# Sequence matrices stored as pairs of tiles: one 512 KB load for two tiles in the first mixing layer of an FNet and GEGLU stack

## The chip, the cores and the metric

The kernel runs on one core of one Trainium2 chip. The metric is the device time of one execution in microseconds (us). Lines named L126 and the like are lines of the kernel before; lines of the changed kernel are said to be such.

## What is computed

Four layers on x (2048 rows of 512 numbers, float32), each added to its input after a layer norm without weights: a Fourier mixing, a GEGLU feed-forward, and both once more.

```python
def _A_ref(x, dft_seq_re, dft_seq_im, dft_hid_re, dft_hid_im):
    a = jnp.einsum("bsd,ed->bse", x, dft_hid_re)
    b = jnp.einsum("bsd,ed->bse", x, dft_hid_im)
    y = jnp.einsum("ts,bse->bte", dft_seq_re, a) - jnp.einsum("ts,bse->bte", dft_seq_im, b)
    return y
def _B_ref(x, w_gate, w_up, w_down):
    return (_gelu(x @ w_gate) * (x @ w_up)) @ w_down
...
x = x + _A_ref(_layernorm(x, axis=-1), ...)   # layer 0
x = x + _B_ref(_layernorm(x, axis=-1), ...)   # layer 1
x = x + _A_ref(_layernorm(x, axis=-1), ...)   # layer 2
x = x + _B_ref(_layernorm(x, axis=-1), ...)   # layer 3
```

The sequence matrices are 2048 by 2048, the hidden ones 512 by 512; the feed-forward is 1792 wide.

## The kernel before

**Products.** Every float32 operand is split in two: ScalarE (ACT) rounds it to a high part (L126), VectorE (DVE) subtracts that from the operand and leaves a low part (L128). A product is then three matmuls, high by high, high by low and low by high (`mm3`, L166 to L168). Most have 512 columns. On top of it the large products run by Winograd's scheme, seven block products for eight, so DVE also forms sums and differences of blocks (`plus`, L157, and `minus`, L154). In layers 0 and 2 the left matrix has the real sequence matrix above the imaginary one, cut at half the sequence: A11 and A12 are the two halves of the real one, A21 and A22 those of the imaginary one. The right matrix is the normed x, cut at half the sequence and at half the features.

**Slots.** SBUF has 93 places of 128 by 512 floats (`Slots`, handed out by `sb.get`, given back by `sb.put`), each the tile of one operand. PSUM has eight banks.

**Sequence tiles.** The host cuts each sequence matrix into tiles of 128 (sequence, on the partitions) by 512 (output rows, a block `b` of four). In DRAM (`ws`) a tile lies in one piece of 256 KB, 2 KB on each partition. `items` is the list of all operands in the order in which TensorE (PE) will want them; `load_next` (L302 is its DMA) takes slots for the next item and starts its loads on the queue of SyncE (SP), some items ahead of the split.

**The first stage of layer 0** (`FORE`, run by `fore`) multiplies all four blocks at once with each of the 16 row tiles `j` of x: for each `j` four sequence tiles, each split and used in six matmuls, 24 matmuls a `j`, in eight PSUM banks. In the first eight `j` it is A11 with the first half of x; then A12 with the second half. Meanwhile the rows of x come in (L194) and are normed: statistics on DVE (L531 to L536), with a power on GpSimd (POOL, L535), and the scaling on ACT (L572). After that, block by block, come the stages `S2` (which loads A21 and A22 of the same `k` in one item and sums them, `make_s2`) and `S4`, and the hidden products between them. Layers 1 and 3 (`geglu`) read split weights from DRAM (`wb`, `wc`): they were split in the first layers and stored, seven halves to a row of 14 KB, so that a tile that is read back is a cut of 2 KB from each such row.

**Order.** The code records operations one after another; a scheduler then sets the order on each engine by its own estimates of time, gives out buffers and inserts the waits. Any change of a load can so move instructions on all engines. SP has eight completion counters for its transfers, and a transfer that has to wait for a buffer holds up those behind it on SP.

## Time and profile before

| | us |
|---|---|
| median of 3 runs | 1589.22 (1588.48 to 1590.95) |
| the profiled execution | 1589.32 |
| its span, first to last instruction | 1587.3 |
| PE busy | 1579.0 |
| DVE busy | 1250.1 |
| ACT busy | 875.4 |
| POOL busy | 253.6 |

The span is what the profile's instructions cover; 2.0 us of the execution's time lie around it. TensorE's granted clock is full through nearly all of the span. DMA moved 427.04 MB, 269 GB/s on the mean. A row such as `12.71 0.50 PE L166 ... [0.75 <-ACT s L126]` reads: started at 12.71 us, took 0.50 us, and the engine sat idle 0.75 us before it until an ACT instruction of line 126 released it. Matmuls overlap: each shows about 0.39 us, and they start some 0.23 us apart. In order listings a tile is named by its place or kind and a running number: `s_735` is a slot's tile, `d_613` a tile of a pair in the changed kernel, `p` a PSUM bank, and `wide` and `xwide` are four-slot tiles that are lent out as slots.

### The profile page before, as it was taken

The page shows a single profiled execution, that of the slowest core. Times are in us where ns is not written, and L with a number is a line of the kernel's source. Part 1 is how long each engine was busy: PE and PEld are TensorE (multiplying, and loading weights), DVE is VectorE, ACT ScalarE, POOL GpSimd, SP SyncE. Part 2 cuts the span into 40 slices and gives each one's busy share as a digit, 9 for nine tenths or more (in the row PEclk, how much of TensorE's full clock was granted, in tenths as well). Part 3 has the DMA queues.
Part 4 walks back from the last instruction along what each step waited for, and adds up shares of the span by engine and source line. Part 5 has one row for each costly group of instructions (what it writes and reads, how often), then busy time and mean ns, then how long its engine had stood idle before and what let it go on. Part 6 is the DMA issues. An engine that isn't in the chain of part 4 may idle for free.

```text
span 1587.3 us, 23208 instructions
## 1 busy us (share of the span) xinstructions
PE 1579.0 (99%) x7000; PEld 1307.6 (82%) x7000; DVE 1250.1 (79%) x2174; ACT 875.4 (55%) x1714; POOL 253.6 (16%) x445
## 2 busy tenths in 40 slices
PE   9999999999999999999999999999999999999998
PEld 7888888888888888888888888888888888888887
DVE  8999999889699795566969997869985458754475
ACT  7864574645676652746768444566546435433361
POOL 2200324311465201230031000021002000000001
PEclk9999999999999999999999999999999999999999
DMA  9946989987999999996976785789998967896463
GB/s 360 332 150 232 361 270 362 335 286 259 328 344 345 297 329 301 288 331 221 310 238 217 270 229 172 233 283 309 279 327 239 297 198 238 293 289 197 135 197 81
DMA packets 257660, 427.04 MB, mean 269 GB/s; under 512 B 33344, under 2 KB 89408, under 8 KB 256512
## 3 DMA queue, kind: packets, MB, share of 16 engines
q1 hardware_dynamic: 228560, 333.28, 66.2%
q0 software_dynamic: 26544, 91.51, 15.7%
q8 instruction: 55, 0.90, 0.2%
q10 hardware_dynamic: 2432, 0.79, 0.2%
q14 instruction: 69, 0.57, 0.1%
HBM read 335.02 MB, written 90.44 MB: 268 GB/s over the span
## 4 chain that ended last, share of the span: by engine, by line
PE 96%; DVE 2%; DMA 2%; issue 0%; ACT 0%; SPq 0%; DVEq 0%; ACTq 0%
PE p L166 32%; PE p L167 32%; PE p L168 32%; DMA s<-ws 1%; DVE s L128 1%; DVE s L154 0%; DMA s<-x 0%; DVE s L157 0%; DVE xwide L154 0%; ACT s L126 0%; DVE wide L154 0%; SPq L302 0%; SPq L194 0%; ACT s L572 0%; DVE wide L157 0%
## 5 line engine op out<-in xcount | busy, mean ns | idle before, releaser
L167 PE MATMUL p<-s,s 128*128 128x512 f32 x2326 | 899.8, 388 | 0.0
L168 PE MATMUL p<-s,s 128*128 128x512 f32 x2326 | 887.6, 388 | 0.0
L166 PE MATMUL p<-s,s 128*128 128x512 f32 x2326 | 872.5, 388 | 2.0 <-ACT s L126 1.5
L126 ACT ACTIVATE s<-s 128x512 fp32r<-128x512 f32 (+1 forms) x868 | 487.4, 608 | 319.8 <-DVE s L154 108.7
L128 DVE TENSOR_TENSOR s<-s,s 128x512 fp32r<-128x512 f32 (+1 forms) x868 | 546.0, 669 | 58.2 <-ACT s L126 54.0
L166 PEld LDWEIGHTS p<-s,s 128*128 128x128 f32 x2326 | 436.7, 188 | 94.2 <-ACT s L126 3.4
L167 PEld LDWEIGHTS p<-s,s 128*128 128x128 f32 x2326 | 436.8, 188 | 89.7 <-DVE s L128 0.5
L168 PEld LDWEIGHTS p<-s,s 128*128 128x128 f32 x2326 | 436.6, 188 | 89.4
L157 DVE TENSOR_TENSOR s<-s,p 128x512 f32<-128x512 f32 (+1 forms) x293 | 196.2, 682 | 189.6 <-PE p L168 109.5
L154 DVE TENSOR_TENSOR s<-s,s 128x512 f32<-128x512 f32 (+1 forms) x414 | 249.8, 623 | 2.8 <-DMA s<-ws 0.9
L161 ACT ACTIVATE s<-p 128x512 f32<-128x512 f32 x252 | 146.9, 592 | 147.0 <-PE p L168 142.0
L1079 ACT ACTIVATE s<-s 128x512 f32<-128x512 f32 x112 | 70.3, 629 | 121.5 <-DVE s L157 121.0
L247 POOL DMA_DIRECT2D x<-wide x16 | 10.4, 660 | 374.7 <-DVE wide L157 374.7
L285 POOL DMA_DIRECT2D wb<-s x84 | 45.9, 548 | 100.2 <-ACT s L126 73.3
L1093 DVE TENSOR_TENSOR s<-s,s 128x512 f32<-128x512 f32 x84 | 57.9, 689 | 1.9
L126 ACT ACTIVATE s<-xwide 128x512 fp32r<-128x512 f32 (+1 forms) x52 | 31.0, 613 | 27.5 <-DVE xwide L157 10.0
L572 ACT ACTIVATE s<-s,shift,rstd 128x512 f32<-128x512 f32 x55 | 44.0, 807 | 3.9 <-DVE shift L536 3.2
L157 DVE TENSOR_TENSOR s<-s,s 128x512 f32<-128x512 f32 (+1 forms) x68 | 40.1, 591 | 5.0 <-DMA s<-wgu 3.3
L545 POOL TENSOR_SCALAR rstd<-rstd 128x1 f32<-128x1 f32 x48 | 14.2, 296 | 179.9 <-ACT junk L544 179.1
L285 POOL DMA_DIRECT2D wc<-s x42 | 30.1, 718 | 74.8 <-ACT s L126 53.2
L128 DVE TENSOR_TENSOR s<-xwide,s 128x512 fp32r<-128x512 f32 (+1 forms) x52 | 35.0, 682 | 7.1 <-ACT s L126 7.0
L542 ACT ACTIVATE junk<-s 128x512 f32<-128x512 f32 x45 | 28.1, 623 | 18.7 <-DMA s<-x 18.4
(105 smaller groups left out, 526.8 us busy)
## 6 DMA issues: line engine op xcount, KB each, us to landing
s<-ws SPq DMA_DIRECT2D x348, 256.0 KB, 5.1
s<-wb SPq DMA_DIRECT2D x294, 256.0 KB, 5.4
s<-wc SPq DMA_DIRECT2D x196, 256.0 KB, 4.5
wb<-s POOLq DMA_DIRECT2D x98, 256.0 KB, 5.6
s<-wp SPq DMA_DIRECT2D x56, 256.0 KB, 4.0
wc<-s POOLq DMA_DIRECT2D x49, 256.0 KB, 5.7
s<-x SPq DMA_DIRECT2D x45, 256.0 KB, 5.3
xwide<-x SPq DMA_DIRECT2D x43, 256.0 KB, 8.0
```

The costliest lines, as they stand in the source:

```text
L126: nc.scalar.activation(hi, src, AF.Copy)
L128: nc.vector.tensor_tensor(lo, src, f32(hi), op=ALU.subtract)
L154: nc.vector.tensor_tensor(out, a, b, op=ALU.subtract)
L157: nc.vector.tensor_tensor(out, a, b, op=ALU.add)
L161: nc.scalar.activation(v, src, AF.Copy)
L166: nc.tensor.matmul(ps, ah, bh, start=start, stop=False, skip_group_check=True)
L167: nc.tensor.matmul(ps, ah, bl, start=False, stop=False, skip_group_check=True)
L168: nc.tensor.matmul(ps, al, bh, start=False, stop=stop, skip_group_check=True)
L285: nc.gpsimd.dma_start(to, t)
L572: nc.scalar.activation(z, x, AF.Identity, bias=shift, scale=rstd)
L1079: nc.scalar.activation(t, g, AF.Gelu_apprx_tanh)
L1093: nc.vector.tensor_tensor(t, t, v, op=ALU.mult)
```

## The change

**In DRAM** the host now lays sequence tiles in pairs: `wf` holds, for the first stage, blocks 0 and 1 (and 2 and 3) of one `j` side by side, 4 KB on each partition; `ws` holds for the real matrix the tiles `k` and `k+1` of a block side by side, and for the imaginary one A21 and A22 of the same `k`. Each is a view of 128 by 1024.

**In SBUF** four pairs of slots (`Pairs`, `d0` to `d3`) take the place of eight slots. The halves of a pair are handed out singly too, but while `sb.reserved` is set (the first stage from `j` = 6 on, and the rest of layer 0) other requests take them last. `get_two` hands out both halves of a free pair where there is one, for float32 alone.

**Loads.** From `j` = 6 on the first stage, and the A21 and A22 item of `S2` in layer 0, go through `Twin`: with a free pair, one transfer of 512 KB fills both tiles; without one, two transfers of 256 KB read the two halves of the view. Everything else reads half a view: 2 KB from each 4 KB. Split weights and hidden weights that happen to lie in the two halves of a pair are joined as well (`kept`, `piece_load`, `load_next`). Of SP's 1493 transfers 36 are saved: 14 joined loads from `wf`, 21 from `ws`, and one of a feed-forward weight. DVE, ACT, PE and POOL's DMAs keep their numbers of instructions.

```diff
+NPAIR = 4
+RESERVE_AT = 6
+JOINED_FROM = 6
...
+    class Pairs(Slots):
+        def __init__(self, pool, n, pairs):
+            super().__init__(pool, "s", n - 2 * pairs)
+            self.free += [(i, h) for i in range(pairs) for h in range(2)]
+            self.kinds, self.reserved = {}, False
...
+            fit = [n for n in self.free if fits(n)]
+            n = next((n for n in fit if not (self.reserved and self.paired(n))), fit[0])
...
+        def get_two(self, dtype=F32):
+            whole = [n for at, n in enumerate(self.free) if self.paired(n) and n[0] not in self.kinds and (n[0], 1 - n[1]) not in self.free[at + 1:]]
+            if dtype != F32 or not whole:
+                return self.get(dtype), self.get(dtype)
+            return self.half_of((whole[0][0], 0), dtype), self.half_of((whole[0][0], 1), dtype)
...
+    class Twin:
+        def __init__(self, view):
+            self.view, self.tiles = view, []
+        def load(self, i):
+            if not self.tiles and not i:
+                self.tiles = list(sb.get_two())
+                both = sb.joined(*self.tiles)
+                for to, a in zip((both,) if both is not None else self.tiles, (self.view,) if both is not None else halves(self.view)):
+                    stream["last"] = nc.sync.dma_start(to, a)
+            return self.tiles[i]
...
-                    for c in range(FORE[layer]):
-                        raw(plain, ws[c * 2 * NS + j])
+                    for c in range(0, FORE[layer], 2):
+                        view = wf[c // 2, j]
+                        two = halves(view) if j < JOINED_FROM else ((twin := Twin(view), 0), (twin, 1))
+                        for a in two:
+                            raw(plain, a)
...
+            low = [Twin(ws[b * NS + NK + k]) for k in range(NK)]
+            high = [a for k in range(NK) for a in halves(ws[b * NS + k])]
+            a11, a12 = high[:NK], high[NK:]
+            a21, a22 = ([halves(twin.view)[i] if layer else (twin, i) for twin in low] for i in range(2))
...
             for j in range(NS):
+                sb.reserved = j >= RESERVE_AT
...
+        sb.reserved = layer == 0 and NPAIR > 0
```

On SP, in the first stage, these rows stand in a row before (the loads from `ws` are the sequence tiles of `j` = 6 and 7, those from `x` rows of x):

```order
L302 DMA s_413<-ws 128x512
L302 DMA s_438<-ws 128x512
L302 DMA s_463<-ws 128x512
L302 DMA s_478<-ws 128x512
L194 DMA s_450<-x 128x512
L194 DMA s_425<-x 128x512
L302 DMA s_496<-ws 128x512
L302 DMA s_521<-ws 128x512
L302 DMA s_536<-ws 128x512
L194 DMA s_508<-x 128x512
```

And now, from the same row of the queue on (L398 and L194 of the changed kernel are `load_next` and `Twin.load`, L273 is the load of a row of x):

```order
L398 DMA s_413<-wf 128x512
L398 DMA s_438<-wf 128x512
L194 DMA d_463<-wf 128x1024
L273 DMA s_450<-x 128x512
L273 DMA s_425<-x 128x512
L194 DMA d_494<-wf 128x1024
L273 DMA d_506<-x 128x512
L194 DMA s_530<-wf 128x512
L194 DMA s_531<-wf 128x512
L273 DMA s_567<-x 128x512
```

The two loads of a pair have become one row twice as wide; a row of x has taken half of the fourth pair, and the next two sequence tiles (`s_530`, `s_531`) are therefore loaded singly. Up to here the order of loads is that of before.

On PE, where `j` = 8 begins (second half of x, first bank `p1`), the order before is as follows; the first name behind the arrow is the part of the sequence tile, the second that of x:

```order
L168 MATMUL p0_232<-s44_727,s31_654 128x512
L166 MATMUL p1_225<-s51_745,s84_490 128x512
L167 MATMUL p1_225<-s55_746,s84_490 128x512
L168 MATMUL p1_225<-s51_745,s84_490 128x512
L166 MATMUL p1_225<-s74_835,s21_613 128x512
```

And now:

```order
L247 MATMUL p0_232<-s42_715,s26_646 128x512
L245 MATMUL p1_225<-s44_735,s82_488 128x512
L245 MATMUL p2_226<-s44_735,s82_488 128x512
L246 MATMUL p1_225<-s61_736,s82_488 128x512
L247 MATMUL p1_225<-s44_735,s82_488 128x512
```

The second matmul of the tile (its low part, `s_746` before, `s_736` now) is put one matmul later. It stands at row 195 of PE's list before and at row 196 now.

On DVE the low part `s_746` stands at row 86 of before:

```order
L531 BN_STATS st<-s_548 128x6
L536 SCALAR_TENSOR_TENSOR shift<-mv,rstd 128x1
L128 TENSOR_TENSOR s_746<-s_619,s_745 128x512
L128 TENSOR_TENSOR s_771<-s_642,s_770 128x512
L533 BN_AGGR mv<-st 128x2
```

The low part `s_736`, of the first joined tile of `j` = 8, stands at row 121 now (L207 of the changed kernel is L128 of before, L233 is L154, L632 to L637 are the statistics):

```order
L632 BN_STATS st<-s_786 128x6
L233 TENSOR_TENSOR s_937<-s_436,s_937 128x256
L207 TENSOR_TENSOR s_809<-s_797,s_809 128x256
L207 TENSOR_TENSOR s_812<-s_797,s_812 128x256
L634 BN_AGGR mv<-st 128x2
L233 TENSOR_TENSOR s_940<-s_436,s_937 128x256
L233 TENSOR_TENSOR s_1055<-s_332 128x256
L635 TENSOR_SCALAR rstd<-mv 128x1
L207 TENSOR_TENSOR s_736<-d_613,s_735 128x512
L233 TENSOR_TENSOR s_1058<-s_672,s_332 128x256
L207 TENSOR_TENSOR s_759<-d_613,s_758 128x512
```

Statistics, splits of rows of x and first differences of x, which before stood behind it, now stand ahead of it: 35 more of DVE's rows come before the low part that PE needs first in `j` = 8. From row 77 to row 121 there are now 5 splits of 512 columns, 12 of 256, 5 differences of 256, 5 statistics (BN_STATS), 6 BN_AGGR, 6 TENSOR_SCALAR and 6 SCALAR_TENSOR_TENSOR.

More of the change, by code (lines that the diff above doesn't have):

```diff
@@ new lines, in fnet_geglu @@
+    class Twin:
[8 more added lines that the diff above has]
+            return self.tiles[i]
+    sb = Pairs(slots, NSLOT, NPAIR)
@@ L279, in kept @@
     def kept(place, parts, by_name=False):
+        both = sb.joined(*parts)
+        if both is not None and not by_name:
+            nc.gpsimd.dma_start(place, both)
+            return
         for n, t in enumerate(parts):
@@ L480, in mix_items @@
                     else:
-                        raw(plain, a22[k])
+                        raw(plain, halves(low[k].view)[1])
             elif what == "PAIR":
@@ L1065, in piece_load @@
     def piece_load(n, i):
-        tiles = [sb.get(F32R) for _ in range(2 if i < 3 else 1)]
-        for k, t in enumerate(tiles):
-            at = i * 1024 + k * 512
-            nc.sync.dma_start(f32(t), wblocks[n][:, at:at + 512])
+        tiles = sb.get_two(F32R) if i < 3 else (sb.get(F32R),)
+        place = wblocks[n][:, i * 1024:i * 1024 + len(tiles) * 512]
+        both = sb.joined(*tiles) if i < 3 else None
+        if both is not None:
+            nc.sync.dma_start(both, place)
+        else:
+            for k, t in enumerate(tiles):
+                nc.sync.dma_start(f32(t), place[:, k * 512:(k + 1) * 512])
         piece_here(n, i, tiles)
```

74 lines of the change are left out of this document (64 added, 10 removed).

## The prediction

> **What bounds the kernel now.** I read the page first, then the waits of PE, then windows by stage, then PE's timeline at its gaps.
>
> ```profile
> span 1587.3 us, 23208 instructions
> PE 1579.0 (99%) x7000; PEld 1307.6 (82%) x7000; DVE 1250.1 (79%) x2174; ACT 875.4 (55%) x1714; POOL 253.6 (16%) x445
> ...
> PE p L166 <- ACT s L126: 1.5, 3, 0.8
> PE p L1368 <- POOL ident masks.py:199: 1.4, 1, 1.4
> PE p L166 <- ACT s L1411: 0.5, 1, 0.5
> ...
> 50.00:880.00 830.00, 830.00 (x3663) 686.88 (x3662) 693.17 (x1234) 503.26 (x1011) 203.23 (x355) 1.00 0.86 291
> ```
>
> PE is busy for 99%, and its waits (time in total, times, longest) are three of ACT's split, 1.5 us, and two before the first product. In the window from 50 to 880 us it is busy for every microsecond. A busy PE need not be a full one, so I look at the distance between starts.
>
> ```profile
> 28.06 1.98 PE L168 MATMUL p<-s,s 128*128 128x512 f32 x8
> ...
> L167 PE MATMUL p<-s,s 128*128 128x512 f32 x2298 | 892.0, 390 | 0.0
> L167 PE MATMUL p<-s,s 128*128 128x256 f32 x28 | 7.8, 283 | 0.0
> ...
> 1581.97 0.28 PE L167 MATMUL p<-s,s 128*128 128x256 f32 x1
> 1582.09 0.28 PE L168 MATMUL p<-s,s 128*128 128x256 f32 x1
> ```
>
> Eight matmuls take 1.98 us, and one 0.39: the distance is (1.98 - 0.39) / 7 = 0.227 us. The long window says the same: 830.00 / 3663 = 0.2266. The three lines have 3 x 2298 = 6894 such matmuls, 1562.9 us at 0.2267, and 84 half as wide, 0.12 us apart by the last two rows, 10.1 us. The first product starts at 6.02 us:
>
> ```profile
> 6.02 0.50 PE L166 MATMUL p<-s,s 128*128 128x512 f32 x1 [0.54 <-ACT s L1411]
> ...
> 12.71 0.50 PE L166 MATMUL p<-s,s 128*128 128x512 f32 x1 [0.75 <-ACT s L126]
> ...
> 24.30 0.50 PE L166 MATMUL p<-s,s 128*128 128x512 f32 x1 [0.37 <-ACT s L126]
> ...
> 920.34 0.47 PE L166 MATMUL p<-s,s 128*128 128x512 f32 x1 [0.35 <-ACT s L126]
> ```
>
> 6.0 + 1562.9 + 10.1 = 1579.0 us would be the end without a lost moment; the last matmul's slot ends at 1582.2. So PE loses 3.2 us in all, most of it in the first 30 us, where it waits and then starts slowly (0.50 instead of 0.39 us). Behind that the one wait is that at 920 us, 0.35 us. **This 3.2 us is all that a change of loads can gain**, unless it changes the 6.0 us ahead of the first product or the 5.1 us behind the last one. That is 0.2% of the time, about what a measurement of this kernel can tell from no change.
>
> **The change part by part.**
>
> *The first 30 us.* Loads, splits and matmuls stand in the old order up to row 30 of SP. What differs is that each 2 KB is cut from 4 KB. The page's issues (count, KB each, us from issue to landing) have such cuts already:
>
> ```profile
> s<-ws SPq DMA_DIRECT2D x348, 256.0 KB, 5.1
> s<-wb SPq DMA_DIRECT2D x294, 256.0 KB, 5.4
> s<-wc SPq DMA_DIRECT2D x196, 256.0 KB, 4.5
> ...
> t<-wide POOLq DMA_DIRECT2D x8, 1024.0 KB, 7.5
> ```
>
> `wb` and `wc` are cut by 2 KB from rows of 14 KB and land in 5.4 and 4.5 us, around the 5.1 us of the solid tiles. I take 0. The ends: two exposed loads (the waits at 12.71 and 24.30 us) that land 0.3 us later or 0.6 us earlier by those rows, so +0.6 to -1.0 us (0.6 of the 0.75 us, and the 0.37).
>
> *Fewer transfers.* 36 issues leave SP. SP computes nothing; what counts is whether somebody waits for a landing. Windows of the start, of the first stage and of the rest of layer 0's mixing (PE, PEld, DVE, ACT and POOL busy, clock, DMA share, GB/s), and the waits for loads in the second and third, show that:
>
> ```profile
> 6.00:28.00 22.00, 20.86 (x88) 16.37 (x89) 19.91 (x48) 17.44 (x33) 3.90 (x5) 1.00 1.05 385
> 28.00:44.00 16.00, 16.00 (x71) 12.93 (x71) 15.94 (x45) 13.76 (x27) 3.23 (x5) 1.00 1.06 387
> 44.00:92.00 48.00, 48.00 (x213) 39.77 (x212) 46.61 (x108) 37.22 (x72) 8.21 (x11) 1.00 0.79 276
> ...
> ACT s L126 <- DMA s<-ws: 1.0, 1, 1.0
> ...
> DVE s L157 <- DMA s<-ws: 1.8, 2, 1.0
> ```
>
> Until 44 us DMA is saturated at 385 to 387 GB/s with transfers of 256 KB, and only two of the joined loads stand among SP's first 50 transfers. From 44 to 92 us ACT waits for a sequence tile once, 1.0 us, and from 92 to 330 us DVE waits twice, 1.8 us; PE in these windows never waits. What the joins save is worth 0; at best the 1.8 us of DVE, none of which reached PE.
>
> The Trainium skill's page "DMA: Bandwidth & Descriptors" says in its section "Bandwidth" that transfers should be batched to a megabyte and more, since smaller ones fall well short of peak, and its section on the anatomy of one DMA puts about 2.0 us of fixed cost on each; by that, 36 joins would be worth an estimated 72 us of DMA time. The trace disagrees: 256 KB loads run at 385 GB/s, since several are in flight.
>
> *A joined load frees both halves only at its end.* 512 KB has no row. Bounds are 5.1 us (256 KB) and 7.5 us (1024 KB); at 386 GB/s the second half takes 0.68 us, so I take 5.8, nearest to the 256 KB row. The first half is so split up to 0.7 us later, by bounds 0 to 2.4. This lies in ACT's and DVE's lead over PE, unless that is gone.
>
> *A joined load waits for a whole pair*, and on SP the rows of x and single tiles behind it wait too; POOL's and ACT's queues keep their transfers. In the first stage `d_690` waits for a matmul itself: the one that gives its buffer back stands 77 ahead of the first that reads its split, 77 x 0.227 = 17.5 us. It needs 5.8 us to land and a split on each of two engines:
>
> ```profile
> L126 ACT ACTIVATE s<-s 128x512 fp32r<-128x512 f32 (+1 forms) x868 | 487.4, 608 | 319.8 <-DVE s L154 108.7
> L128 DVE TENSOR_TENSOR s<-s,s 128x512 fp32r<-128x512 f32 (+1 forms) x868 | 546.0, 669 | 58.2 <-ACT s L126 54.0
> ```
>
> 5.8 + 0.6 + 0.7 = 7.1 us; the other 10.4 are room for what is queued ahead on ACT and DVE. I take 0; without that room each microsecond over it would be one on PE.
>
> *DVE's order in the first stage.* This is the step with a price. DVE is busy for 46.61 of 48 us, nearly full. Before, the low part of the first tile of `j` = 8 stands at row 86 of DVE, now at row 121, while PE wants it at the same place. The rows of DVE's timeline, between row 75 and row 121 of before:
>
> ```profile
> 36.48 0.15 DVE L536 SCALAR_TENSOR_TENSOR shift<-mv,rstd 128x1 f32<-128x1 f32 x1
> 36.54 0.69 DVE L128 TENSOR_TENSOR s<-s,s 128x512 fp32r<-128x512 f32 x1
> 37.14 0.18 DVE L533 BATCH_NORM_AGGREGATE mv<-st 128x2 f32<-128x6 f32 x1
> ...
> 37.88 0.15 DVE L534 TENSOR_SCALAR rstd<-mv 128x1 f32<-128x1 f32 x1
> 37.95 0.69 DVE L128 TENSOR_TENSOR s<-s,s 128x512 fp32r<-128x512 f32 x1
> 38.54 0.69 DVE L531 BATCH_NORM_STATS2 st<-s 128x6 f32<-128x512 f32 x1
> 39.15 0.15 DVE L536 SCALAR_TENSOR_TENSOR shift<-mv,rstd 128x1 f32<-128x1 f32 x1
> ...
> 49.15 0.76 DVE L128 TENSOR_TENSOR s<-s,s 128x256 fp32r<-128x256 f32 x2
> 49.88 0.42 DVE L154 TENSOR_TENSOR s<-s,s 128x256 f32<-128x256 f32 x1
> 50.21 0.42 DVE L154 TENSOR_TENSOR s<-s 128x256 f32<-128x256 f32 x1
> 51.08 0.16 DVE L536 SCALAR_TENSOR_TENSOR shift<-mv,rstd 128x1 f32<-128x1 f32 x1 [0.44 <-POOL rstd L535]
> ...
> 52.36 0.39 PE L168 MATMUL p<-s,s 128*128 128x512 f32 x1
> ```
>
> From start to start a split of 512 columns holds DVE 0.60 us (36.54 to 37.14), one of 256 0.34 (0.76 - 0.42, two in a row), a difference 0.33, a statistic 0.61, the small ones 0.09 (BN_AGGR, taken from 37.14 to the split behind it), 0.07 and 0.06. Rows 77 to 121 are now 5 x 0.60 + 12 x 0.34 + 5 x 0.33 + 5 x 0.61 + 6 x (0.09 + 0.07 + 0.06) = 13.1 us, from about 36.5 us on: `s_736` is ready at 49.6 us. If each of its 6 shifts waits 0.44 us for POOL, as at 51.08 us, it is 52.2. PE reaches row 196 at 52.36 us, the last row above. So the lead falls from about 12 us (row 86 of before starts 0.06 us behind the shift at 39.15 and takes 0.69: done by 39.9; its first reader is the matmul ahead of that at 52.36) to between 0.2 and 2.8 us. I take 1.5: no wait, but one landing that is 2 us late makes one. The wait that I expect is 0.6 us, from bounds of 0 and 2.2 (2.4 for a load late by the worst bound, less 0.2).
>
> *The other stages.* Rows move there too, with the same numbers of instructions and the same scheduler. The narrowest stage is that before 920 us:
>
> ```profile
> 840.00:925.00 85.00, 84.65 (x373) 69.76 (x373) 85.00 (x155) 50.92 (x95) 6.36 (x12) 1.00 0.77 255
> ```
>
> DVE has no free moment in 85 us, and PE's 0.35 us is what comes of it. A new order can save that or add as much as one or two of DVE's 0.60 us steps: -0.35 to +1.2 us. I take 0.
>
> **Sum.** 0 + 0 + 0.6 + 0 = +0.6 us on the profiled execution's 1589.32 (span 1587.3 and 2.0 around it): 1589.9. That execution lies 0.1 above the median of the three runs, so I say 1589.8. The bounds together are -1.0 - 0.35 = -1.4 and 0.6 + 2.2 + 1.2 = +4.0 us; not all ends meet.
>
> **The rivals.**
>
> *Slower: PE runs into DVE at j = 8 and stays there.* The lead that is gone at 52 us isn't rebuilt, since DVE is full (46.61 of 48 us), and each of the joined loads that follow (12 of the 14 in the first stage) makes PE wait for the late first half, up to 0.68 us: 12 x 0.68 = 8.2 us at most; half of it is +4.1, 1593.3. It decides where `s_736` is ready later than 52.4 us by more than once, that is, if DVE also loses some 2.8 us to landings on its way. For it: the 35 rows put ahead, and that a tile's split can't start before its transfer has ended. Against it: ACT waited for a sequence tile only once in this stage. And once the norms are over, DVE has less to do. I give 13%.
>
> The Trainium skill's page "DMA: Bandwidth & Descriptors", section on the anatomy of one DMA, states that a transfer's semaphore fires only when its last byte is confirmed to have landed. No row of before has two halves in one transfer, so the trace can't say yet what that costs.
>
> *Faster: the loads were what held PE.* If joined loads arrive so much earlier that every wait goes, the time falls by the 3.2 us above, to 1586.1. Against it: most of that is lost before 30 us, ahead of the first split of a joined load. 2%. (The batching rule of the Trainium skill's page "DMA: Bandwidth & Descriptors", section "Bandwidth", cited above, would have it so.)
>
> *It doesn't do what it says.* Pairs are rarely free: 14 of 20 possible joins in the first stage, 21 of 32 later; weights are joined once. Then nothing happens but a new order. That is inside my forecast, whose sum has 0 for the joins.
>
> **How the numbers follow.** My forecast, no change that can be told, 85%: 1589.8, by itself 1588.0 to 1592.0. Slower by over 0.2% is beyond 1592.4, faster beyond 1586.0. The slower rival's half price is 1593.3; to 1593.0 the range takes in its lower part. The low end is the lower sum, 1589.2 - 1.4 = 1587.8, and the lowest of three runs was 1588.48, so 1588.0. Range 1588.0 to 1593.0; faster 0.02, same 0.85, slower 0.13.
>
> **What would show it.** Right: PE's waits stay a few rows, with at most one new one between 50 and 70 us of under 1 us; PE busy near 1579; 35 rows `d<-wf` and `d<-ws` of 512 KB that land in about 5.8 us; single loads still in 5.1. Wrong in the first step: the waits at 12.71 and 24.30 us change by more than 0.3 us. Wrong in the third: PE waits for DVE L207 or ACT L205 of the changed kernel more than twice between 50 and 92 us, or DVE idles for `DMA d<-wf` there. A time under 1588 would mean that PE's start or tail moved, which nothing here explains.

## The result, and the profile after

The changed kernel took 1598.36 us (median of 6 runs, 1596.95 to 1601.82), the kernel before 1589.35 us beside it: a ratio of 1.0051, with a 95% interval of 1.0041 to 1.0061. The prediction was 1589.8 us, in a range of 1588.0 to 1593.0. The profiled execution took 1598.09 us.

The page of the changed kernel, its span and busy times, and the waits of PE (in total, times, longest):

```profile
span 1596.3 us, 22925 instructions
PE 1582.2 (99%) x7000; PEld 1309.9 (82%) x7000; DVE 1254.3 (79%) x2174; ACT 875.3 (55%) x1714; POOL 257.3 (16%) x445
...
PE p L245 <- ACT s L205: 6.8, 3, 6.1
PE p L1476 <- POOL ident masks.py:199: 1.3, 1, 1.3
PE p L245 <- ACT s L240: 0.7, 1, 0.7
PE p L246 <- DVE d L207: 0.5, 1, 0.5
```

The span is 9.0 us longer, and of PE's waits one alone is 6.1 us. To see where the 9 us arise I compare the starts of matmuls of the same number in the two timelines. The changed kernel is 0.3 us ahead at 28 us, 0.6 ahead at 330, 0.6 late at 838 (behind the wait for ACT L240), 0.1 late at 1060, and 9.2 late at 1145; from there to the end it stays 9.1 to 9.2 late. So the whole loss of this execution lies between 1060 and 1145 us, in layer 2, where no load is joined. PE's timeline there, with its two idle times in brackets (the first ends at PE's 4841st matmul):

```profile
1101.18 0.39 PE L247 MATMUL p<-s,s 128*128 128x512 f32 x1
1107.66 1.22 PE L245 MATMUL p<-s,s 128*128 128x512 f32 x2 [6.10 <-ACT s L205]
1109.35 0.80 PE L246 MATMUL p<-d,s 128*128 128x512 f32 x1 [0.47 <-DVE d L207]
1109.94 0.63 PE L247 MATMUL p<-s,s 128*128 128x512 f32 x1
1110.37 0.63 PE L246 MATMUL p<-d,s 128*128 128x512 f32 x1
1110.80 0.63 PE L247 MATMUL p<-s,s 128*128 128x512 f32 x1
...
1112.90 0.40 PE L246 MATMUL p<-s,s 128*128 128x512 f32 x1
1113.13 0.40 PE L247 MATMUL p<-s,s 128*128 128x512 f32 x1
```

Two matmuls should start 0.227 us apart; from 1101.18 to 1107.66 it is 6.48, so 6.25 us are lost there. After that they stand 0.43 us apart (1109.94, 1110.37, 1110.80) until 1112.90, and the windows give the clock (the column behind POOL):

```profile
1085.00:1101.00 16.00, 16.00 (x73) 13.23 (x72) 12.13 (x21) 7.78 (x17) 2.73 (x4) 1.00 1.09 266
1101.00:1107.00 6.00, 0.56 (x3) 0.14 (x1) 4.00 (x7) 1.80 (x4) 0.00 (x0) 0.92 1.01 342
1107.00:1113.00 6.00, 4.87 (x11) 3.41 (x12) 6.00 (x11) 2.99 (x5) 0.00 (x0) 0.51 0.86 249
```

In the last window PE does 11 matmuls, where 26 would fit 0.227 us apart, at 0.51 of the clock. Together with the 0.47 us wait this restart costs the rest, 9.1 - 6.25 = 2.9 us. What PE waited for, followed back: ACT's split waited for a sum of DVE, and DVE for sequence tiles. DVE's idle times in this place:

```profile
1086.41 0.69 DVE L236 TENSOR_TENSOR s<-d,s 128x512 f32<-128x512 f32 x1 [0.78 <-DMA s<-ws]
1101.60 0.69 DVE L236 TENSOR_TENSOR s<-s,s 128x512 f32<-128x512 f32 x1 [3.69 <-DMA s<-ws]
1104.99 0.69 DVE L233 TENSOR_TENSOR s<-s,s 128x512 f32<-128x512 f32 x1 [1.31 <-DMA s<-ws]
```

The loads in question stand in SP's queue among four loads of layer 2's x, 256 KB each in 512-byte runs, that nothing reads before 1170 us. The queue of the changed kernel (start, time, instruction):

```profile
1083.71 0.37 SPq L313 DMA_DIRECT2D xwide<-x  x1
1084.13 0.48 SPq L398 DMA_DIRECT2D s<-ws  x1
1084.66 0.84 SPq L313 DMA_DIRECT2D xwide<-x  x1
1086.40 0.33 SPq L337 DMA_DIRECT2D s<-m  x1
1086.82 0.38 SPq L398 DMA_DIRECT2D s<-ws  x1
1087.70 0.32 SPq L313 DMA_DIRECT2D xwide<-x  x1
1089.44 1.32 SPq L398 DMA_DIRECT2D s<-ws  x2
1091.70 0.33 SPq L313 DMA_DIRECT2D xwide<-x  x1
```

In the kernel before the same four stood earlier:

```profile
1075.77 0.39 SPq L234 DMA_DIRECT2D xwide<-x  x1
1076.74 4.36 SPq L234 DMA_DIRECT2D xwide<-x  x3
```

DMA in the meantime (the last two columns: share and GB/s), after and, below, before:

```profile
1087.00:1098.00 11.00, 11.00 (x50) 9.10 (x49) 10.91 (x19) 5.14 (x10) 1.76 (x3) 1.00 1.14 223
```

```profile
1087.00:1098.00 11.00, 11.00 (x51) 9.10 (x50) 10.96 (x19) 5.09 (x9) 1.09 (x2) 1.00 1.05 385
```

The DMA engines were as busy, but moved 223 instead of 385 GB/s. Of the sequence tiles issued between 1080 and 1110 us the changed kernel had 16 in single slots, which landed in 7.3 us (and 2 in halves of pairs), and the kernel before 20, in 5.4:

```profile
s<-ws SPq DMA_DIRECT2D x16, 256.0 KB, 7.3
xwide<-x SPq DMA_DIRECT2D x4, 256.0 KB, 10.0
```

```profile
s<-ws SPq DMA_DIRECT2D x20, 256.0 KB, 5.4
```

The places that the prediction named as likely to cost look like this after the change: the stage with the joined loads, the one long wait for such a load, and the joined loads themselves (count, KB, us to landing):

```profile
44.00:92.00 48.00, 48.00 (x213) 39.74 (x213) 46.57 (x103) 37.93 (x74) 8.30 (x9) 1.00 0.77 273
```

```profile
ACT s L205 <- DMA d<-wf: 3.1, 1, 3.1
```

```profile
s<-ws SPq DMA_DIRECT2D x225, 256.0 KB, 5.2
d<-ws SPq DMA_DIRECT2D x21, 512.0 KB, 5.2
s<-wf SPq DMA_DIRECT2D x36, 256.0 KB, 5.5
d<-wf SPq DMA_DIRECT2D x14, 512.0 KB, 6.5
```

PE is busy for all of the 48 us, whatever the joined loads did.

### The profile page after: what moved, and what is told of

It is laid out like the page before. It is cut to its first block, busy times and chain, and to the rows that moved or that the text cites. A ratio compares the mean times of both kernels' runs of the same rounds, so it can differ in the third digit from the quotient of the medians.

```text
span 1596.3 us, 22925 instructions
## 1 busy us (share of the span) xinstructions
PE 1582.2 (99%) x7000; PEld 1309.9 (82%) x7000; DVE 1254.3 (79%) x2174; ACT 875.3 (55%) x1714; POOL 257.3 (16%) x445
## 3 DMA queue, kind: packets, MB, share of 16 engines
q0 software_dynamic: 26544, 91.51, 15.6%
## 4 chain that ended last, share of the span: by engine, by line
PE 97%; DMA 1%; ACT 1%; DVE 0%; SPq 0%; issue 0%; POOL 0%; DVEq 0%; POOLq 0%
PE p L245 33%; PE p L246 32%; PE p L247 32%; DMA s<-m_sum 1%; ACT s L205 0%; DMA s<-wf 0%; DVE s L207 0%; ACT s L673 0%; SPq L398 0%; DVE st L632 0%; SPq L273 0%; DVE s L233 0%; DVE d L207 0%; DVE s L236 0%; ACT s L240 0%
## 5 line engine op out<-in xcount | busy, mean ns | idle before, releaser
L246 PE MATMUL p<-s,s 128*128 128x512 f32 (+1 forms) x2089 | 808.2, 388 | 0.0
L247 PE MATMUL p<-s,s 128*128 128x512 f32 (+1 forms) x2066 | 790.6, 388 | 0.0
L245 PE MATMUL p<-s,s 128*128 128x512 f32 x2016 | 752.7, 389 | 7.5 <-ACT s L205 6.8
L205 ACT ACTIVATE s<-s 128x512 fp32r<-128x512 f32 (+1 forms) x672 | 382.7, 604 | 237.6 <-DVE s L233 88.4
L246 PEld LDWEIGHTS p<-s,s 128*128 128x128 f32 x2089 | 392.6, 188 | 80.9 <-DVE s L207 0.4
L207 DVE TENSOR_TENSOR s<-s,s 128x512 fp32r<-128x512 f32 (+1 forms) x636 | 406.9, 668 | 62.7 <-ACT s L205 59.6
L247 PEld LDWEIGHTS p<-s,s 128*128 128x128 f32 x2066 | 388.3, 188 | 79.4
L245 PEld LDWEIGHTS p<-s,s 128*128 128x128 f32 x2016 | 379.2, 188 | 87.2 <-ACT s L205 8.4
L236 DVE TENSOR_TENSOR s<-s,p 128x512 f32<-128x512 f32 x259 | 174.8, 685 | 157.5 <-PE p L247 76.5
L240 ACT ACTIVATE s<-p 128x512 f32<-128x512 f32 x228 | 133.6, 592 | 110.9 <-PE p L247 105.8
L233 DVE TENSOR_TENSOR s<-s,s 128x512 f32<-128x512 f32 (+1 forms) x294 | 179.3, 624 | 5.8 <-DMA s<-ws 4.1
L205 ACT ACTIVATE s<-d 128x512 fp32r<-128x512 f32 (+1 forms) x143 | 85.8, 618 | 51.8 <-DVE d L233 13.9
L207 DVE TENSOR_TENSOR s<-d,s 128x512 fp32r<-128x512 f32 (+1 forms) x142 | 96.1, 688 | 5.9 <-ACT s L205 5.5
L247 PE MATMUL p<-d,s 128*128 128x512 f32 x202 | 78.1, 389 | 0.0
L245 PE MATMUL p<-d,s 128*128 128x512 f32 x192 | 72.8, 389 | 0.0
L246 PE MATMUL p<-d,s 128*128 128x512 f32 x119 | 46.9, 394 | 0.5 <-DVE d L207 0.5
```

The lines of the kernel that those rows point to most:

```text
L205: nc.scalar.activation(hi, src, AF.Copy)
L207: nc.vector.tensor_tensor(lo, src, f32(hi), op=ALU.subtract)
L233: nc.vector.tensor_tensor(out, a, b, op=ALU.subtract)
L236: nc.vector.tensor_tensor(out, a, b, op=ALU.add)
L240: nc.scalar.activation(v, src, AF.Copy)
L245: nc.tensor.matmul(ps, ah, bh, start=start, stop=False, skip_group_check=True)
```

## The experiments

All times are medians, with the ratio to the kernel before that ran beside them and its 95% interval. "Late at" is the start of a matmul less that of the same number in the profiled kernel before. The last columns come from one profiled execution of each kernel, which need not be a typical one: it took 1594.90 us for the split joins, whose other three took 1600.26 to 1601.67, 1590.80 for two pairs and 1593.86 for S3 on GpSimd. Small differences in them mean little: `late_x` and its control have the order of the kernel that they were made from up to 1076 and 1072 us, and yet are 2.1 and 2.7 us later than it at 1060. The 4751st matmul is the one that starts at 1081 us in the kernel before.

| kernel | us | ratio (95%) | late at 330 / 838 / 1060 / 1145 us | DVE instructions, 1060 to 1101 us | DVE instructions done by the 4751st matmul |
|---|---|---|---|---|---|
| before, 94 slots | 1588.48 | 0.9988 (0.9978-0.9997) | -0.9 / -0.9 / -1.1 / -1.1 | 63 | 1632 |
| before, 93 slots | 1589.35 | | 0 | 60 | 1633 |
| before, x later | 1591.35 | 1.0004 (0.9995-1.0014) | 1.6 / 1.6 / 2.7 / 2.8 | 57 | 1633 |
| layout only | 1591.43 | 1.0005 (0.9996-1.0014) | 1.0 / 1.0 / 0.6 / 3.1 | 59 | 1633 |
| two pairs | 1593.30 | 1.0020 (1.0008-1.0033) | -0.3 / 0.0 / 1.2 / 1.1 | 59 | 1633 |
| before, DVE work added | 1594.01 | 1.0019 (1.0009-1.0030) | -0.5 / -0.5 / 0.7 / 4.8 | 60 | 1633 |
| three pairs | 1595.80 | 1.0040 (1.0022-1.0057) | 1.2 / 1.2 / 5.8 / 6.0 | 51 | 1631 |
| younger half | 1596.08 | 1.0035 (1.0021-1.0048) | -0.5 / 3.0 / 2.4 / 6.8 | 50 | 1629 |
| x later | 1596.17 | 1.0034 (1.0022-1.0046) | -0.6 / 0.6 / 2.2 / 8.0 | 56 | 1628 |
| S3 on GpSimd | 1596.63 | 1.0036 (1.0023-1.0049) | -0.2 / 1.0 / 0.7 / 5.1 | 54 | 1627 |
| x later, S3 on GpSimd | 1597.12 | 1.0040 (1.0025-1.0055) | -0.7 / 1.2 / 2.7 / 7.8 | 48 | 1628 |
| changed | 1598.36 | 1.0051 (1.0041-1.0061) | -0.6 / 0.6 / 0.1 / 9.2 | 52 | 1628 |
| own halves, 94 slots | 1600.52 | 1.0062 (1.0050-1.0075) | -0.4 / 0.2 / 0.0 / 10.7 | 45 | 1628 |
| joins split | 1600.73 | 1.0055 (1.0035-1.0075) | -0.4 / 0.8 / 0.2 / 6.2 | 55 | 1629 |
| changed, 94 slots | 1600.73 | 1.0063 (1.0046-1.0079) | 0.1 / 7.6 / 10.8 / 12.6 | 49 | 1632 |
| before, 95 slots | 1604.68 | 1.0094 (1.0079-1.0109) | 7.5 / 8.0 / 7.4 / 15.6 | 41 | 1632 |
| changed, 95 slots | 1605.32 | 1.0100 (1.0080-1.0120) | 1.5 / 1.5 / 6.0 / 11.9 | 48 | 1631 |
| own halves | 1607.28 | 1.0100 (1.0086-1.0114) | 2.4 / 2.6 / 4.7 / 12.9 | 45 | 1629 |
| own halves, joins split | 1607.78 | 1.0103 (1.0090-1.0117) | 3.7 / 5.6 / 6.9 / 15.9 | 41 | 1628 |
| before, 92 slots | 1608.58 | 1.0111 (1.0096-1.0126) | 3.8 / 4.2 / 6.2 / 20.2 | 38 | 1629 |

**Were it the x loads?** My first theory was the queue above: the four loads of x, put among urgent ones. `late_x` and its control on the kernel before issue them behind the last sequence load:

```
             elif b - 1 in PAIRED[layer]:
...
-                for g in (b - 1, b):
-                    load_turned(layer, g)
+                with tc.issue_after(stream["last"].ins) if b == NB - 1 else nullcontext():
+                    for g in (b - 1, b):
+                        load_turned(layer, g)
```

> The changed kernel with one thing put later: the loads of layer 2's x for its last pair of blocks (four of 512-byte runs, xwide, and the wide ones beside them) are issued behind the last sequence load that has been issued, instead of in among the sequence loads of the stage S2 of block 3. Nothing reads them for another 60 us or more. Theory (the stall at 1101 us comes from these four slow transfers taking DMA time and places in SP's queue when sequence tiles are due): the wait of 6.1 us and PE's slow restart go, PE has at most 1 us of waits between 1090 and 1110 us, and the time falls by about 9 to 1589 to 1590.5 us. Rival (the sequence tiles of that stage are late by themselves, because their slots come free later in the new order, or because of the m and m_sum reloads and the 1 MB store): PE still waits 4 to 6 us there and the time stays 1595 to 1599 us.

> The kernel before with the same x loads of layer 2's last pair put behind the last sequence load issued; a control. Theory (in the kernel before these loads come early enough not to collide, and PE has 3.2 us of loss in all): 1588 to 1590.5 us, nothing gained or lost that a measurement can tell. Rival (putting them later is a gain by itself, with or without the pairs): under 1586 us; or they now come late for their own readers: over 1592.5 us with a PE wait near 1160 to 1180 us.

The wait at 1101 us went, and the same window of 1087 to 1098 us has 372 GB/s again. But the time fell by some 2 us, not 9. PE now waited 22 us further on (and 1.1 us at 922, where the edit has changed nothing yet):

```profile
1126.81 0.77 PE L245 MATMUL p<-s,s 128*128 128x512 f32 x1 [2.68 <-DVE s L236]
```

```profile
1127.00:1133.00 6.00, 6.00 (x15) 4.65 (x16) 4.55 (x8) 2.92 (x5) 0.00 (x0) 0.51 0.85 250
```

So the stall at 1101 us goes when these loads are moved, and up to 1076 us every engine's order is that of the changed kernel. They don't make it by themselves: in `s3_on_pool`, below, they stand among the sequence loads too, whose tiles land in 7.5 us, and PE doesn't wait there. That they made the loss is refuted. The control neither gained nor lost what can be told.

**Joins or layout?** The one makes each joined load of a sequence matrix as two, into the same halves; the other has no pair slots (`NPAIR = 0`).

```
-                for to, a in zip((both,) if both is not None else self.tiles, (self.view,) if both is not None else halves(self.view)):
+                for to, a in zip(halves(both) if both is not None else self.tiles, halves(self.view)):
```

> The changed kernel with its pair slots and its order kept, but each sequence load that was joined is made as two transfers of 256 KB into the two halves. Theory (the cost sits at 1101 us, where no load is joined; the joins themselves are worth nothing): the stall stays, 1597 to 1599.5 us, and PE's waits before 330 us differ by under 1 us from the changed kernel's. Rival (the joins are what costs, by halves that come late or transfers that shift everything behind them): 1589 to 1591 us.

> The changed kernel with no pair slots at all, so that no load is joined and only the layout in DRAM is new (each tile of 256 KB is cut by 2 KB out of rows of 4 KB). PE's order is that of the kernel before, those of DVE and ACT differ from it in a hundred rows or so. Theory (the layout costs nothing, the loss comes from the order that the pair slots bring about in layer 2): 1588.5 to 1591 us, sequence loads of 256 KB still landing in 5.0 to 5.4 us at the median, no PE wait over 1 us after 30 us. Rival (cutting by 2 KB out of 4 KB makes the loads slower, and layer 2 is where it shows): 1594 to 1599 us, and a PE wait of several us near 1100 us.

Two transfers for one change nothing that can be told: 1.0055 against 1.0051, with intervals that overlap. The first is wide, some 3 us to either side, and the order isn't quite kept: DVE's list differs in 285 of 2174 places, PE's in 8. The layout alone costs nothing that can be told either, though its profile has a wait of 2.27 us just behind that stage, at 1124.77 us: PE's order there is the old one, the order on DVE and ACT isn't.

**How much room has that stage?** In `before_dve8` the low part of 8 splits is computed twice in S2 of block 3. The two others have S3 on GpSimd, with x later and without.

```
-            return split_slot(a11)
+            hi, lo = split_slot(a11)
+            if b == NB - 1 and not keep:
+                nc.vector.tensor_tensor(lo, a11, f32(hi), op=ALU.subtract)
+            return hi, lo
```

```
-            minus(a21, a11, a21)
+            (nc.gpsimd if b == NB - 1 and not keep else nc.vector).tensor_tensor(a21, a11, a21, op=ALU.subtract)
```

> The kernel before, where in the stage S2 of block 3 of layer 2 the low part of each of 8 splits is computed twice: 8 more DVE instructions of 0.69 us, 5.5 us, no other work; PE's order is the same. Theory (that stage had no slack in the kernel before either: DVE idles for 5 us between 1060 and 1115 us, all of it ahead of 1085, and PE gets there with under 0.5 us to spare): PE waits 3 to 5.5 us in all between 1095 and 1130 us, with a stretch at half clock behind it where one wait is over 2.5 us, so 1593.5 to 1598.5 us. Rival (DVE has room there, and the loss of the changed kernel is due to its loads or pair slots alone): PE's waits stay under 1 us, 1588.5 to 1591 us.

> The changed kernel with only the second of these two edits: S3 of layer 2's block 3 on GpSimd, the x loads where they were. Theory (both resources have no slack there: at 1101 us it was a sequence tile that had not landed, and DVE had nothing to do, so less work for DVE doesn't help): PE still waits 3 us or more at about 1101 us, 1595 to 1599 us. Rival (DVE's work alone is the limit, and the late loads are a symptom of slots that DVE frees late): the wait goes and the time is 1589 to 1591 us.

> The changed kernel with the x loads of layer 2's last pair put later (as in the run before), and in the stage S2 of block 3 of layer 2 the difference S3, one of three sums per tile, done by GpSimd instead of VectorE: 8 times 0.69 us = 5.5 us less for DVE. Theory (with the loads out of the way that stage is bound by DVE, which is full from 1095 to 1115 us; PE's 2.7 us of wait at 1123.7 us and the slow restart behind it are DVE's backlog): no PE wait over 0.5 us between 1090 and 1130 us, no stretch at half clock, and the time falls from 1596.2 by the 6.4 us that this place cost, to 1589 to 1591 us. Rival (the stage waits for its loads, or GpSimd's slower sums put PE off in their place): a PE wait of 2 us or more stays there, 1594 to 1598 us.

`before_dve8` took 1594.01 us, 1.0019 (1.0009 to 1.0030). At the end of that stage its PE waits once, 2.20 us, and restarts slowly; it is 0.7 us late at 1060 and 4.8 at 1145. So 5.5 us of added DVE work made a wait of 2.2 us, which shows that DVE's lag alone can stop PE here; there are some 3 us of room, more than the theory had, whose 3 us of waits at least weren't reached. With the slow restart the 2.2 us cost 4.1, and the time is the theory's, not the rival's.

The GpSimd runs took 1596.63 us (1.0036, 1.0023 to 1.0049) and 1597.12 us (1.0040, 1.0025 to 1.0055), with 2.29 and 2.31 us of wait and a slow restart. Both theories missed: `s3_on_pool` has no wait at 1101 us (its time is where the theory had it), and `late_x_s3_pool` isn't cured, as its rival had it. The sums are slow on GpSimd and slow DVE down beside them. GpSimd and DVE of `s3_on_pool`:

```profile
1107.83 1.62 POOL L458 TENSOR_TENSOR s<-s,s 128x512 f32<-128x512 f32 x1 [3.94 <-DMA s<-t]
```

```profile
1107.62 0.69 DVE L207 TENSOR_TENSOR s<-s,s 128x512 fp32r<-128x512 f32 x1
1108.45 1.54 DVE L207 TENSOR_TENSOR s<-s,d 128x512 fp32r<-128x512 f32 x1 [0.15 <-ACT d L205]
```

DVE's split of 0.69 us takes 1.54 while GpSimd adds. These two runs don't tell whether less work on DVE would have helped.

**Another order without pairs.** The kernel before with one number changed (`NSLOT = 93` to 92, 94 or 95): no pairs, the old layout, the same work.

> The kernel before with 92 slots instead of 93 and nothing else: no pairs, the old layout; only the order in which slots come free, and with it the order of loads and sums, is another. Theory (what the change cost is an accident of the order in a stage without slack, so another order without pairs can cost as well): PE's waits change by a microsecond or more in some stage of layer 2 or of layer 0, wherever they come; time 1588 to 1598 us. Rival (pairs or joined loads themselves cause the loss, and a mere change of the order costs nothing): no PE wait over 1 us after 30 us, 1588.5 to 1591 us.

> The kernel before with 94 slots instead of 93. Theory (the order alone decides, and one slot more can't make the loads later on the whole): 1587.5 to 1592 us, PE's waits in layer 2 under 2.5 us, unlike the 1608.6 us of 92 slots. Rival (the number of slots is nothing but another accident): as likely over 1592 us as under it.

> The kernel before with 95 slots. Theory (slots are short in layer 2; more of them let VectorE stand further ahead when the narrow stage begins): 1587 to 1589.5 us as with 94, and between 1060 and 1101 us DVE has done 60 instructions or more. Rival (the order alone): anywhere, as likely over 1590.7 us as under.

One slot less costs 18 us, one more gains 2, and two more cost 15. At 92 slots the largest of its waits, in PE's timeline, has the mark of the changed kernel, in layer 2 too, but a stage earlier (a second one of 4.11 us ends at 1140.24):

```profile
1079.07 0.79 PE L166 MATMUL p<-s,s 128*128 128x512 f32 x1 [5.34 <-DVE s L157]
1079.66 0.63 PE L167 MATMUL p<-s,s 128*128 128x512 f32 x1
1080.08 0.63 PE L168 MATMUL p<-s,s 128*128 128x512 f32 x1
```

With 95 it waits 3.14 us at 213 us and 2.81 at 1136. With 92 the missing slot may have its part; with 95 none is missing, so a new order alone can cost more than the change did. More slots are no cure either: the theory that slots are short falls with the 95.

**More or fewer pairs.** `NPAIR` is 2 or 3, or it stays 4 and `NSLOT` is 94 or 95.

> The changed kernel with two pairs of slots instead of four. Theory (an accident of the order): the time doesn't follow the number of pairs; it is set by the wait in layer 2's S2 of block 3 (1095 to 1130 us), whatever it comes to, and PE loses under 1 us more than before ahead of 330 us. Rival (the cost goes with the pairs): about half of the change's 9 us, 1593 to 1595 us.

> The changed kernel with three pairs of slots. Theory: as with two pairs, not on a line between 0 pairs (1591.4 us) and 4 pairs (1598.4 us). Rival (the cost goes with the pairs): three quarters of 9 us, 1595 to 1597 us, and more than with two pairs.

> The changed kernel with 94 slots instead of 93 (four pairs as before, one single slot more), nothing else. Theory (pairs and joined loads cost nothing themselves; the loss is the place where the order of layer 2 lets one stage run dry, and one more slot gives another order and a little more lead): the wait at 1101 us is another, and the whole is anywhere from 1588 to 1600 us, with no loss before 330 us above 1 us. Rival (pairs, by halves that are held for each other, slow every order): over 1594 us here too, with a PE wait of several us in layer 2's S2 of block 3.

> The changed kernel with 95 slots, four pairs among them. Theory (pairs are worth fewer slots than they hold, two more make up for part): 1590 to 1596 us, DVE with 53 to 60 instructions between 1060 and 1101 us. Rival (with pairs each order is a bad one, whatever the number of slots): 1597 us or more, and at most 52 instructions there.

With 2, 3 and 4 pairs the medians rise, 1593.3, 1595.8 and 1598.4 us, as if the pairs cost. But the traces don't share a place: three pairs lose 4.1 us between 838 and 945 us (its longest wait, 2.71 us, ends at 851.87) and 0.2 between 1060 and 1145, where the changed kernel loses all. With 94 slots four pairs took 1600.73 us, some 7 us late by 838 us already, and with 95 slots 1605.32. Here the rivals did better than my expectations: no version with more than two pairs has a median under 1595 us.

**The other half of a pair.** That made me look at what a pair costs by itself. It is one buffer, made anew each time that both halves are free, so a half waits for the readers of the other half too. For each first use of a half in the changed kernel I took from the trace when the last readers of either half ended, and when the engine was done with what stood ahead: some 34 waits of over 0.3 us are due to the other half alone, some 87 us in all, more than half of it on SP. SP's queue at the longest:

```profile
1465.12 0.32 SPq L398 DMA_DIRECT2D s<-wc  x1
1476.48 0.80 SPq L1177 DMA_DIRECT2D d<-wb  x2
```

The half that is loaded at 1476.48 had not been in use; the readers of the other ended at 1476.44. Two edits take such waits away. In one a pair is one buffer for the whole program, for raw tiles alone; in the other an older half is passed over until the younger one's turn. The first was also run with its joined sequence loads as two transfers, and with 94 slots.

```
-            if i not in self.kinds:
-                self.kinds[i] = self.pool.tile([P, 1024], dtype, name=f"d{i}"), dtype
+            if i not in self.always:
+                self.always[i] = self.pool.tile([P, 1024], F32, name=f"d{i}"), F32
+            self.kinds.setdefault(i, self.always[i])
...
-                    return n[0] not in self.kinds or self.kinds[n[0]][1] == dtype
+                    return dtype == F32
```

```
             fit = [n for n in self.free if fits(n)]
+            fit = [n for n in fit if not self.younger(n)] or fit
...
+        def younger(self, n):
+            return self.paired(n) and n[0] not in self.kinds and (n[0], 1 - n[1]) in self.free[self.free.index(n):]
```

> The changed kernel where each pair of slots is one buffer for the whole program instead of a new one each time that both halves are free, so that a half waits for its own readers alone; such halves take raw F32 tiles only, not the split parts. All 43 joins stay, PE's order is that of the kernel before but for four rows near the end. Theory (b, the loss is the wait for the other half's readers): no PE wait over 1 us between 840 and 1140 us, 1588.5 to 1591.5 us. Rival (a, an accident of the order): the orders of SP and DVE are again others, the time is anywhere, as likely over 1593 us as under.

> The same kernel as own_halves_f32, but each sequence load that is joined there is made as two transfers of 256 KB into the two halves; PE's order is the same. Theory (joined transfers are worth nothing by themselves, since several transfers are in flight anyway): within 1.5 us of own_halves_f32. Rival (fewer, longer transfers are a gain once their slots cost nothing): 2 us or more slower than own_halves_f32.

> The changed kernel with one rule more: the older half of a free pair is passed over while another slot fits, so that a half is taken only where the younger half's turn has come, and its readers are done as early as a single slot's would be. Halves still take both kinds of tiles. Theory (b): waits for the other half's readers fall from 87 us to under 20 us, and the time from 1598.4 to 1589 to 1593 us. Rival (a): the time stays 1595 to 1600 us though those waits are gone.

> own_halves_f32 with 94 slots instead of 93. Theory: as the kernel before with 94 slots, 1587.5 to 1590 us, since the joins add nothing; PE waits of under 0.6 us after 30 us. Rival (joined loads gain where nothing else is in the way): under 1586.5 us; or (an accident of the order): over 1592 us.

Waits for the other half fell to none and to 30 us, and the time didn't come back: 1607.28 us with own halves, 1600.52 with 94 slots, 1596.08 with the younger half. Each of these edits deals a new order too, so by themselves they don't prove the waits harmless; but in the changed kernel none of over 0.6 us ends between 1042 and 1107 us, where the 9 us are lost. And with own halves, joined or split makes 1607.28 or 1607.78 us (1.0103, with 1.0090 to 1.0117): once more a joined load is worth nothing that can be told.

**What the runs agree on.** The order of the work alone can move the time by more than the change did, with pairs and without. PE's waits in this part of layer 2 stand mostly at the same matmuls from kernel to kernel. At the 4841st, within S2 of block 3, where the changed kernel loses its 6.1 us, four kernels wait, 1.76 to 6.10 us. At the 4931st, some 20 us further on, twelve do, 0.64 to 4.52 us, `late_x`, `layout_only` and `before_dve8` among them. This is the first matmul of S4: it goes on in a PSUM bank that S2 has filled, and in nine of the twelve what ends the wait is DVE's sum that reads such a bank (L157 of before). The changed kernel, held up long at the first, doesn't wait at the second; `late_x` took the first wait away and met the second.

What goes with the loss is how far DVE has come by then. The window from 1060 to 1101 us (PE, PEld, DVE, ACT and POOL busy), in the kernel before, in the changed one, and in that before with 92 slots:

```profile
1060.00:1101.00 41.00, 41.00 (x183) 33.97 (x182) 36.14 (x60) 30.33 (x75) 9.63 (x18) 1.00 0.97 307
```

```profile
1060.00:1101.00 41.00, 41.00 (x183) 33.94 (x182) 32.17 (x52) 30.70 (x76) 9.46 (x18) 1.00 0.93 262
```

```profile
1060.00:1101.00 41.00, 35.66 (x150) 29.04 (x149) 23.52 (x38) 30.29 (x75) 7.49 (x17) 0.92 0.84 249
```

DVE did 60 instructions before, 52 after and 38 with 92 slots, where PE waits inside the window already. 8 fewer, at 0.60 us from start to start, are 4.8 us of work that is still to be done. In the table the kernels with 57 or more lose at most 2.5 us between 1060 and 1145, but for the one with DVE work added (4.1), and those with 56 or fewer 4.4 to 14.0 us, but for two: three pairs (0.2) and the changed kernel with 94 slots (1.8). These two come to the stage 5.8 and 10.8 us late, so that a window fixed in time meets them at an earlier point of the work.

The last column counts up to the same matmul instead, ahead of the wait at the 4841st, and has the two in their place. All ten kernels in which DVE has done 1627 to 1629 instructions by then lose 4.4 us or more. Of the ten with 1631 to 1633 seven lose at most 2.5; the others are the one with DVE work added behind that point, and the two with 95 slots (5.9 and 8.2), which this count doesn't explain. The changed kernel, with 1628 against 1633, falls behind just before, from 1070 to 1080 us (before, then changed):

```profile
1070.00:1080.00 10.00, 10.00 (x46) 8.29 (x45) 10.00 (x17) 8.64 (x23) 3.02 (x5) 1.00 1.00 305
```

```profile
1070.00:1080.00 10.00, 10.00 (x46) 8.29 (x45) 7.45 (x13) 8.95 (x25) 3.78 (x7) 1.00 0.99 296
```

DVE is busy for 7.45 of 10 us there, where it was full before: it waits 1.59 us for ACT's scaling of x (L673 of the changed kernel) and 0.83 us for a sequence tile. The first of the four x loads is issued at 1083.71 us, so the lag is older than they are.

What stays open is whether pairs lead to bad orders more often than any other edit does: that the changed kernel's loss is an accident of its order is argued from what the runs exclude; no run has the pairs with the order of before. Each of the twelve kernels with three pairs or four took over 1595 us, but so did two of the three other slot counts without pairs. 93 and 94 slots give good orders; no run tells why.

## Why the prediction was wrong

- *The first 30 us*: right by its ends, +0.6 to -1.0 us. The two waits, with 0.75 and 0.37 us, are now these:

```profile
12.45 0.50 PE L245 MATMUL p<-s,s 128*128 128x512 f32 x1 [0.29 <-ACT s L205]
...
24.03 0.50 PE L245 MATMUL p<-s,s 128*128 128x512 f32 x1 [0.41 <-ACT s L205]
```

  The first is 0.46 us shorter, more than the 0.3 that I had set as a sign of error; PE was 0.6 us ahead at 330 us, and the gain was gone by 838.
- *Fewer transfers*: right at 0. The changed kernel against its form with two transfers, and own halves against theirs, differ by less than the intervals, and PE, which sets the time, waits for none of these loads. The batching rule of the Trainium skill's page "DMA: Bandwidth & Descriptors", section "Bandwidth", found no support in either pair of runs. Nor did the 72 us of DMA time, which the prediction had estimated from the fixed cost on the same page; the page gives both for transfers issued from GpSimd, and these are issued from SP.
- *A joined load frees both halves only at its end*: I took 5.8 us, from bounds of 5.1 and 7.5; the rows have 6.5 (14 of them) and 5.2 (21). ACT waited 3.1 us for one, PE for none.
- *A joined load waits for a whole pair*: I took 0 for the joined loads. I overlooked that single tiles in halves wait as well, 87 us in all. What that is worth to PE stays 0 as far as the runs show.
- *DVE's order in the first stage*: the mechanism was right, its 0.6 us of wait was not. The low part that I expected to be ready at 49.6 to 52.2 us is this one, done at 50.18:

```profile
49.49 0.69 DVE L207 TENSOR_TENSOR s<-d,s 128x512 fp32r<-128x512 f32 x1
```

  PE took it at 52.0, and was 0.6 us ahead at 330 us. The rival that PE runs into DVE at j = 8 did not happen.
- *The other stages*: this step failed. I wrote that rows move there too, by the same scheduler, that a new order can save 0.35 or add 1.2 us, and took 0. It added 9.1 us, from one place: 6.25 us of standstill where DVE was five instructions behind, and 2.9 us of slow restart, for which the term had nothing at all. I had sized it by the one visible wait, at 920 us, and by one or two steps of DVE, and looked nowhere for a stage that has little room although PE doesn't wait. Such a stage could have been found in the profile of before: from 1085 to 1115 us DVE is busy for every microsecond, the DMA share is above 1 until 1105, and PE still doesn't wait. That sign isn't sharp: DVE was as full from 840 to 925 us, where the changed kernel lost nothing and three pairs lost 4.1 us.
- *It doesn't do what it says*: I had this as a new order and nothing else, with no cost. As far as the runs show, it was a new order and nothing else, and that was the cost.

## What to carry to other kernels

Where a scheduler and a free list set the order, an edit in one layer re-deals the order of all that follow, and a stage in which DVE and DMA are both full has little room for a worse deal: price such an edit by running the kernel before with one slot more or less, not by the edit's own transfers. A stage without PE waits isn't a stage with room; look for windows in which the engine that feeds PE is busy for 100%. The best version was the kernel before with 94 slots, 0.9988 of its time (0.9978 to 0.9997), and none with pairs.

## What the hardware showed

**The clock after a wait.** Behind a wait PE may run some matmuls 0.427 us apart, at half clock. Of all waits of over 0.6 us in the runs, between 30 and 1575 us, every one of 2.68 us or more (ten of them) was followed by 5 to 13 such matmuls, some 0.2 us of loss for each; of the 31 from 1.1 to 2.66 us nine were. The length alone doesn't tell which: 2.20 us in `before_dve8` brought 7, 2.27 in `layout_only` none. The place does. Within a run the profile's record of the clock changes only at steps of 3.41 us, and half clock lasts one step or two. With PE's idle time counted inside each step, all 16 steps at full clock with 1.99 us or more of it were followed by half clock, three of the four from 1.82 to 1.90 us were, and none with 1.81 us or less. The 2.20 us of `before_dve8` lie within one step; the 2.27 of `layout_only` are cut into 0.5 and 1.75. So one long wait costs more than several short ones of the same sum that fall into different steps.

The Trainium skill's page "TensorE: Matmul & The Clock Gate" warns, in its section "Why this matters for your kernels", of idle gaps of more than about 3 us, and says under "What's actually happening" that the window is free-running. The runs agree with the second, as their steps don't move with the waits; for the first, 1.82 us within one step were enough at times.

**GpSimd beside DVE.** A sum of 128x512 on GpSimd took 1.3 to 2.1 us in the means of its groups, and one of DVE's splits beside it 1.54 instead of 0.69 us.

**Short runs.** The 256 KB loads of x in 512-byte runs landed in 10.0 us (median of the four), and while they were under way, beside a store of 1 MB, DMA moved 223 GB/s at a share of 1.14.
